# Turning attention outputs by DMA in two f16 halves, and rebuilding 64-bit weights in two VectorE passes

## The chip, the core and the metric

The kernel runs on one NeuronCore of a Trainium2 chip. The core has five engines that run their own instruction streams and meet through semaphores: TensorE (PE in the profile; its weight loads are listed as PEld), VectorE (DVE), ScalarE (ACT), GpSimd (POOL) and SyncE (SP), which here issues all DMAs. Matmul results land in PSUM; GpSimd works on SBUF alone in this kernel. The metric is the device time of one execution in microseconds (us). The kernel before takes 1158.41 us, the median of 3 runs (1158.35 to 1158.62).

## What is computed

Attention with queries pooled in pairs, then a gated feed-forward block that mixes each token with the one before it. B = 8 batches, H = 8 heads, S = 1152 keys, 576 pooled queries, D = 64; the model width is 512 and the inner width 1024.

```
q_pool = q.reshape(B, H, S // 2, 2, D).mean(axis=3)
scores = scale * q_pool @ k^T;  attn = softmax(scores);  x_head = attn @ v
x = concat of heads: (8, 576, 512)
x_prev = x shifted by one token (zero at the start of a batch)
xk = mu_k * x + (1 - mu_k) * x_prev;   xr likewise with mu_r
k = relu(xk @ w_k);  v = k * k @ w_v;  r = sigmoid(xr @ w_r);  out = r * v
```

The weights arrive as 64-bit floats. Every float32 product is made of f16 or bf16 pieces (a high part and a low part), so that a product takes three matmuls.

## The kernel before

**Attention.** There are 64 heads (n = 0 to 63, eight to a batch), each of six blocks of 96 queries. A block (`block`) runs through the engines in turn: 9 score matmuls into one of three PSUM buffers `s` (L479), a maximum on VectorE (L486), a small turn on TensorE (L489), a second maximum (L492), a matmul that spreads it (L494), one row written by ScalarE (L497), 9 more matmuls that add the low parts and the maximum (L503), the exponential on ScalarE (L509) into `pf`, and the low part `pl` by GpSimd (L512). The buffer `s` is free again when the exponential has read it. Five windows to a head (`window`) multiply these by `v` into one PSUM bank `a` (L538, L540, L545); at the last window of a head, bank `a` is divided by the row sums into `xb` (L562 to L569).

**The turn.** The feed-forward needs x with channels on partitions. After every second head, `xb` holds 5 pieces of 128 tokens by 128 channels (two heads). TensorE turns them by a product with the identity in two groups, of 3 and of 2 (L581), back into bank `a`, and ScalarE copies each group into `xt` (L584). `xt` has three buffers, one to a batch in turn; the four pairs of a batch fill its groups g = 0 to 3.

**Feed-forward.** 4608 tokens are worked in 18 tiles of 256 (`ff`). `mix` makes xk and xr from `xt`, one channel group c at a time (ScalarE L653, VectorE L656, ScalarE L662, GpSimd L664); then come the products with w_k, w_r and w_v (all L684), with L711 to L748 behind them. A tile can be worked when all four groups of its tokens stand in `xt`.

**Weights.** In the first stage, beside the attention of batch 0, 20 pieces of 128 by 512 weights are rebuilt from their 64-bit words (`weights`): a DMA of 512 KB into one of two staging buffers `st` (L602), ScalarE's scaled absolute value of the upper words into PSUM bank `f` (L613), three VectorE passes (shift L615, sign L616, low bits L618) that end in `ex`, the f16 high part by ScalarE (L620) and the low part by GpSimd (L621). The first two loads (`iss.nw <= 2`) name `ks1`, `ks2` and `vr` of the first heads as read, so they are issued after those are ready.

**What sets the order.** No instruction is issued as written: `op` records each with its engine, an assumed duration, what it reads and writes and a priority (`key`), and `Issue.run` lists all engines' streams, SP's DMA issues among them, by trying list schedules with these durations. Each engine then works its stream strictly in order. A changed duration or a removed instruction thus moves others anywhere.

Of the kernel before, what the change touches and what calls it, by code (L numbers as in the profile page):

```python
# [34 lines left out]
LO, VLO = 2.0 ** -28, 2.0 ** -12  # L35
# [223 lines left out]
def kernel(  # L259
# [63 lines left out]
    kr, vr = bufs("kr", 2, [P, NC, D], F32), bufs("vr", 2, [P, NC, D], F32)  # L323
# [5 lines left out]
    ks1, ks2 = bufs("ks1_", 2, [P, NC, P], F16), bufs("ks2_", 2, [P, NC, P], F16)  # L329
# [5 lines left out]
    cross = const.tile([P, D + 1], F32, name="cross")  # L335
# [3 lines left out]
    xt = bufs("xt", 3, [P, NG, TQ + 1], F32)  # L339
# [119 lines left out]
    def block(n, j, i, t):  # L459
# [22 lines left out]
        for c0, c1 in BK:  # L482
# [11 lines left out]
        op("PE", 0.05, lambda: nc.tensor.matmul(s[:, 0:QN], mbz[0:QN].broadcast_to([QN, P]),  # L494
                                                 negi[0:QN, 0:QN], start=False, stop=False, skip_group_check=True),
           r=[("mb", z)], w=[("s", z)], key=t + O_MAX)
        op("ACT", 0.133, lambda: nc.scalar.activation(qlo[QN:QN + 1], s[QN:QN + 1, 0:QN], AF.Prelu,  # L497
                                                      scale=1.0 - EPS, alpha=(1.0 + EPS) / (1.0 - EPS)),
           r=[("s", z)] + kl, w=kl, key=t + O_MAX)

# [21 lines left out]
    def window(n, w, t):  # L522
# [32 lines left out]
        if w < NW - 1:  # L555
# [3 lines left out]
        z = n % 2  # L559
        dz, xz = den[z], xb[0]  # L560
        up = slice(HALF, P)
        op("ACT", 0.25, lambda: nc.scalar.activation(cross[up], a_b[0:HALF, 0:VN], AF.Copy, scale=VLO),  # L562
           r=[("a",)], w=[("cross",)], key=t + O_EVAC)
        op("DVE", 0.16, lambda: nc.vector.tensor_tensor(a_b[up, 0:VN], a_b[up, 0:VN], cross[up], op=ALU.add),
           r=[("cross",), ("a",)], w=[("a",)], key=t + O_EVAC)
        op("DVE", 0.075, lambda: nc.vector.tensor_scalar(dz, u[:, :, D], GUARD, None, op0=ALU.add),
           r=[("a",)], w=[("den", z)], key=t + O_EVAC)
# [2 lines left out]
            xz[:, :, hh], u[:, :, 0:D], dz.unsqueeze(2).broadcast_to([P, NW, D]), op=ALU.mult),  # L570
           r=[("den", z), ("a",)], w=[("xb", hh)], key=t + O_EVAC)
        if hh == 0:
            return
        for k0, k1 in TURN:
            q0, qe = spans(k0, k1)
# [10 lines left out]
               r=[("a",)], w=[("xt", b % 3, g, k0)], key=t + O_TURN)  # L586


    def weights(n, w, kc, key, step):
        cols = w.shape[1]  # L590
        wv = w.bitcast(I32).rearrange("(c p) (f t) -> c p f t", p=P, t=2)
        for c in range(kc):
            for f in range(0, cols, 512):
                i = iss.nw = getattr(iss, "nw", 0) + 1
                i %= 2
                s3 = st[i].rearrange("p (f t) -> p f t", t=2)
                wl, wh = s3[:, :, 0], s3[:, :, 1]
# [12 lines left out]
                op("ACT", 0.48, lambda u=u, wh=wh: nc.scalar.activation(u, wh.bitcast(F32), AF.Abs, scale=2.0 ** -111),  # L613
                   r=[ks], w=[kf], key=key)
                v_(0.6, lambda ui=ui: nc.vector.tensor_scalar(ui, ui, 3, None, op0=ALU.logical_shift_left), [kf], [kf])  # L615
# [204 lines left out]
```

## Time and profile before

| | value |
|---|---|
| median of 3 runs | 1158.41 us (1158.35 to 1158.62) |
| the profiled execution itself | 1158.5 us |
| its span, first to last instruction | 1156.7 us (1.8 us lie outside) |
| matmuls | 18928, of which 160 are turns (L581) |
| DMA issued from SP's queue | 123.77 MB, 47.1% of 16 engines' span |
| DMA transposes | 66 of queries, 64 of keys |

The page gives busy time by engine. A matmul's duration in it is longer than the distance to the next one, since matmuls overlap; what one costs in TensorE's stream is read from the starts of neighbours in the timeline. The chain of waits is followed back from the last instruction to what released each step. In rows of groups, `out<-in` gives the tiles, `x` the count, then busy us and mean ns, then the idle time before them and its releasers.

### The profile page before, as it was taken

The numbers are of one execution on the slowest core, as the hardware profiler recorded it, in microseconds if no ns is written. First come the engines' busy times: TensorE is split into PE (matmuls) and PEld (weight loads), VectorE is DVE, ScalarE is ACT, GpSimd is POOL, SyncE is SP. The second block draws the span as 40 slices with busy tenths as digits, with TensorE's granted clock in tenths as the row PEclk, the third lists the DMA queues.
The fourth block names the chain that finished last, engine by engine and source line by source line (L and its number), as shares of the span: only waits on it lengthen the run. The fifth ranks groups of instructions, "written<-read, shape, count | busy, mean of one in ns | idle before, by whom it ended". The sixth has DMA issues, their size and how long they took to land.

```text
span 1156.7 us, 44885 instructions
## 1 busy us (share of the span) xinstructions
PE 1105.0 (96%) x18928; PEld 916.0 (79%) x18928; DVE 859.4 (74%) x1622; ACT 875.9 (76%) x1810; POOL 740.0 (64%) x883
## 2 busy tenths in 40 slices
PE   3878889999999999999999999999999999999998
PEld 3767787988889887978788888879797878887565
DVE  6899987888887777787687878777787778673320
ACT  4778888788778787887878786978887788775643
POOL 3767786766767567666767675857666676654431
PEclk9799999999999999999999999999999999999999
DMA  9687655466354644565444444655544444310000
GB/s 225 183 201 183 172 137 138 99 130 133 99 124 104 126 90 111 124 114 115 93 118 97 116 96 110 119 116 102 114 109 104 111 96 93 73 27 11 19 20 28
DMA packets 222378, 126.64 MB, mean 109 GB/s; under 512 B 157664, under 2 KB 194528, under 8 KB 222176
## 3 DMA queue, kind: packets, MB, share of 16 engines
q1 hardware_dynamic: 222176, 123.77, 47.1%
q8 instruction: 148, 2.42, 0.9%
q14 instruction: 54, 0.44, 0.1%
HBM read 67.11 MB, written 9.44 MB: 66 GB/s over the span
## 4 chain that ended last, share of the span: by engine, by line
PE 85%; DVE 5%; ACT 4%; DMA 3%; issue 2%; SPq 1%; ACTq 0%; DVEq 0%
PE f L684 33%; PE s L479 11%; PE s L503 11%; PE a L538 7%; PE a L540 7%; PE a L545 6%; PE s L684 4%; ACT pf L509 2%; DVE mx L486 2%; PE s L489 2%; PE a L684 2%; PE s L494 1%; PE a L581 1%; DMA ks<-kn 1%; DMA kr<-in_k_dram 1%
## 5 line engine op out<-in xcount | busy, mean ns | idle before, releaser
L486 DVE TENSOR_REDUCE mx<-s 128x96 f16<-128x864 f32 x384 | 401.5, 1054 | 107.2 <-PE s L479 59.8
L512 POOL TENSOR_SCALAR pl<-pf 128x864 f16<-128x864 uint16 (+1 forms) x384 | 337.8, 880 | 186.3 <-ACT pf L509 157.9
L509 ACT ACTIVATE pf<-s 128x864 int32<-128x864 f32 x384 | 337.6, 889 | 84.6 <-PE s L503 50.5
L479 PE MATMUL s<-qT,ks 128*128 128x96 f16 x3456 | 217.8, 208 | 25.6 <-ACT pf L509 12.7
L538 PE MATMUL a<-vt,pf 128*128 128x65 f16 x2880 | 230.2, 194 | 1.5 <-ACT pf L509 0.9
L540 PE MATMUL a<-vt,pf 128*128 128x64 f16 x2880 | 230.4, 194 | 0.0
L479 PEld LDWEIGHTS <-ks 128*128 128x128 f16 x3456 | 185.4, 99 | 51.3 <-issue 18.4
L503 PE MATMUL s<-qT,ks 128*128 128x96 f16 x3456 | 215.0, 208 | 7.5 <-ACT qT L497 6.8
L538 PEld LDWEIGHTS <-pf 128*128 128x128 f16 x2880 | 200.5, 99 | 6.3 <-ACT pf L509 1.2
L503 PEld LDWEIGHTS <-ks 128*128 128x128 f16 x3456 | 181.9, 99 | 28.7 <-issue 9.1
L540 PEld LDWEIGHTS <-pf 128*128 128x128 f16 x2880 | 192.4, 98 | 7.7 <-issue 1.0
L492 DVE TENSOR_REDUCE mb<-s 96x1 f16<-96x128 f32 x384 | 109.3, 285 | 79.9 <-PE s L489 71.8
L497 ACT ACTIVATE qT<-s 1x96 f16<-1x96 f32 x384 | 92.1, 242 | 88.4 <-PE s L494 75.7
L684 PE MATMUL f<-xhk,wk_hi 128*128 128x256 f16 x496 | 135.1, 272 | 0.2
L684 PE MATMUL f<-xlk,wk_hi 128*128 128x256 f16 x496 | 135.1, 272 | 0.0
L684 PE MATMUL f<-xhk,wk_lo 128*128 128x256 f16 x496 | 135.1, 272 | 0.0
L545 PE MATMUL a<-vb,pl 128*128 128x65 f16 x2304 | 124.0, 194 | 0.2 <-POOL pl L512 0.2
L684 PEld LDWEIGHTS <-wk_hi 128*128 128x128 f16 x1152 | 107.0, 98 | 11.0 <-issue 0.4
L435 POOL TENSOR_TENSOR kn<-kr,kn 128x320 f16<-128x320 f32 x126 | 99.6, 802 | 17.5 <-ACT kn L430 13.5
L715 POOL TENSOR_TENSOR gl<-g 128x512 f16<-128x512 f32 x72 | 77.3, 1075 | 46.1 <-ACT g L713 43.8
L545 PEld LDWEIGHTS <-pl 128*128 128x128 f16 x2304 | 99.2, 98 | 5.1 <-POOL pl L512 0.5
L489 PE MATMUL s<-identb,mx 128*96 128x128 f16 x384 | 87.6, 228 | 6.8 <-DVE mx L486 6.7
(96 smaller groups left out, 2089.9 us busy)
## 6 DMA issues: line engine op xcount, KB each, us to landing
kr<-in_k_dram SPq DMA_DIRECT2D x64, 288.0 KB, 3.0
vr<-in_v_dram SPq DMA_DIRECT2D x64, 288.0 KB, 3.2
qr<-in_q_dram SPq DMA_DIRECT2D x32, 320.0 KB, 3.4
ks<-ks SPq DMA_DIRECT2D x64, 144.0 KB, 2.5
out_dram<-em SPq DMA_DIRECT2D x36, 256.0 KB, 2.4
qr<-in_q_dram SPq DMA_DIRECT2D x32, 256.0 KB, 3.3
st<-in_moe_w_k_dram SPq DMA_DIRECT2D x8, 512.0 KB, 4.9
st<-in_moe_w_v_dram SPq DMA_DIRECT2D x8, 512.0 KB, 4.6
```

Source lines behind the costliest of these rows:

```text
L435: lambda cs=cs, en=nc.vector if ve else nc.gpsimd: en.tensor_tensor(kn[i][:, cs, D:P], kr[i][:, cs], kn[i][:, cs, 0:D], op=ALU.subtract),
L479: nc.tensor.matmul(cols(c, c + 1), ks1[hp][:, c, :], qhi, start=(c == c0), stop=False, skip_group_check=True)
L486: op("DVE", 0.967, lambda: nc.vector.tensor_reduce(mxz, grid(0, NC).rearrange("p c q -> p q c"), axis=AX.X, op=ALU.max), r=[("s", z)], w=[ ...
L489: op("PE", 0.054, lambda: nc.tensor.matmul(s[0:QN, 0:P], mxz, identb, start=False, stop=False, skip_group_check=True), r=[("mx", z)], w=[( ...
L492: op("DVE", 0.199, lambda: nc.vector.tensor_reduce(mbz[0:QN], s[0:QN, 0:P], axis=AX.X, op=ALU.max), r=[("s", z)], w=[("mb", z)], key=t + O ...
L503: nc.tensor.matmul(cols(c, c + 1), ks2[hp][:, c, :], qlo, start=False, stop=True, skip_group_check=True)
L509: op("ACT", NC * QN / 1200 + 0.051, lambda: nc.scalar.activation(pf[:, :, HALF + rows.start:HALF + rows.stop], grid(0, NC), AF.Exp, bias=S ...
L512: op("POOL", NC * (r1 - r0) / 1000 + 0.066, lambda: nc.gpsimd.tensor_scalar(to, half(pf, U16, 0)[:, :, HALF + r0:HALF + r1], LO, 1.0, op0= ...
L538: nc.tensor.matmul(a_b[:, a0:a0 + VN], half(pf, F16, 1)[:, c, his], vt[jv][:, c, D:D + VN], start=(w == 0 and c == 0), stop=False, skip_gr ...
L540: nc.tensor.matmul(a_b[:, a0:a0 + D], half(pf, F16, 1)[:, c, his], vt[jv][:, c, 0:D], start=False, stop=(side and c == NC - 1), skip_group ...
L545: nc.tensor.matmul(a_b[:, a0:a0 + VN], pl[:, c, rows], vb[jv][:, c, 0:VN], start=False, stop=(c == NC - 1), skip_group_check=True)
L684: nc.tensor.matmul(ps, terms[i][0], terms[i][1], start=(first and i == 0), stop=(i == last), skip_group_check=True)
```

## The change

Three things are done, and three assumed durations of the planner are set anew (0.133 to 0.36 for L497, 0.25 to 0.34 for L562, 0.16 to 0.36 for L564, and 0.48 to 0.52 for L613).

1. **The turn, from batch 1 on (n >= 8).** ScalarE casts `xb` to an f16 high half, GpSimd makes the f16 rest, two DMA transposes turn the halves, and GpSimd adds them into `xt`. The halves live in the two `st` buffers, which the weights no longer need by then. Batch 0 keeps the turn on TensorE.
2. **The weights.** The shift pass and the pass for the low bits become one; the low bits are taken by ScalarE from the top byte of the lower word. So two VectorE passes and one more ScalarE pass a piece.
3. **Staging.** The weights pass through four buffers, two of them in `xt[2]`, which batch 2 is the first to use; a memset restores its zero column. Pieces 3 and 4 fall into buffers of their own, and their loads have no reads named that hold them back.

```diff
+    xbh, xbl, xth, xtl = (st[i].bitcast(F16)[:, o * NW * P:(o + 1) * NW * P] for i in (0, 1) for o in (0, 1))
...
+        if n >= H:
+            flat = "p k h d -> p (k h d)"
+            op("ACT", 0.63, lambda: nc.scalar.copy(xbh, xz.rearrange(flat)),
+               r=[("xb", 0), ("xb", 1)], w=[("xbh",), *old[0]], key=t + O_TURN)
+            op("POOL", NW * P * 0.0019 + 0.09, lambda: nc.gpsimd.tensor_tensor(xbl, xz.rearrange(flat), xbh, op=ALU.subtract),
+               r=[("xb", 0), ("xb", 1), ("xbh",)], w=[("xbl",), *old[0]], key=t + O_TURN)
+            for kx, x, to in (("xbh", xbh, xth), ("xbl", xbl, xtl)):
+                op("DMA", 0.8, lambda x=x, to=to: nc.sync.dma_start_transpose(to.rearrange("p (k x) -> p k x", k=NW), x),
+                   r=[(kx,)], w=[(kx, "t"), *old[1]], key=t + O_TURN, tail=2.0)
+            op("POOL", TQ * 0.0019 + 0.09, lambda: nc.gpsimd.tensor_tensor(
+                xt[b % 3][:, g, 1:1 + TQ], xth[:, HALF:], xtl[:, HALF:], op=ALU.add),
+               r=[("xbh", "t"), ("xbl", "t")], w=[("xt", b % 3, g, k0) for k0, k1 in TURN], key=t + O_TURN, port=True)
+            return
...
+    far = xt[2].rearrange("p c t -> p (c t)").bitcast(I32)
+    stage = [*st, *(far[:, i * 1024:(i + 1) * 1024] for i in range(2))]
...
-                i %= 2
-                s3 = st[i].rearrange("p (f t) -> p f t", t=2)
+                i, j = i % 2, i % len(stage)
+                s3 = stage[j].rearrange("p (f t) -> p f t", t=2)
+                tops = stage[j].bitcast(U8).rearrange("p (f b) -> p f b", b=8)[:, :, 3]
...
-                   r=[("ks1", 1, 0), ("ks2", 0), ("vr", 1)] if iss.nw <= 2 else [], w=[ks], key=key, tail=4.5)
+                   r=[("ks1", 1, 0), ("ks2", 0), ("vr", 1)] if iss.nw <= 2 else [], w=[ks, kl], key=key, tail=4.5)
...
-                v_(0.6, lambda ui=ui: nc.vector.tensor_scalar(ui, ui, 3, None, op0=ALU.logical_shift_left), [kf], [kf])
-                v_(0.6, lambda ui=ui, wh=wh: nc.vector.scalar_tensor_tensor(
-                    ui, wh, -0x80000000, ui, op0=ALU.bitwise_and, op1=ALU.bitwise_or), [ks, kf], [kf])
-                v_(0.6, lambda ei=ei, ui=ui, wl=wl: nc.vector.scalar_tensor_tensor(
-                    ei, wl, 29, ui, op0=ALU.logical_shift_right, op1=ALU.bitwise_or), [ks, kf], [ke])
+                    op("ACT", 0.57, lambda wl=wl, tops=tops: nc.scalar.activation(wl, tops, AF.Copy, bias=-0.49, scale=2.0 ** -5),
+                       r=[ks, kl], w=[kl], key=key)
+                    v_(0.6, lambda ui=ui, wl=wl: nc.vector.scalar_tensor_tensor(
+                        ui, ui, 3, wl, op0=ALU.logical_shift_left, op1=ALU.bitwise_or), [kl, kf], [kf])
+                    v_(0.6, lambda ei=ei, ui=ui, wh=wh: nc.vector.scalar_tensor_tensor(
+                        ei, wh, -0x80000000, ui, op0=ALU.bitwise_and, op1=ALU.bitwise_or), [ks, kf], [ke])
...
+    op("POOL", 0.2, lambda: nc.gpsimd.memset(xt[2][:, :, 0:1], 0.0), w=[(m, j) for m in ("st", "sl") for j in (2, 3)] +
+       [("xt", 2, g, k0) for g in range(NG) for k0, k1 in TURN], key=W_REST * PER + 14 * W_REST_STEP * PER)
```

With these lines in place the line numbers of the changed kernel run ahead by 3 at the attention (L486 becomes L489) and by 25 at the feed-forward (L684 becomes L709).

Three places show how instructions move. The first is SP's stream at the program's start, before:

```order
L392 DMA qr_74<-in_q_dram 128x5x128
L423 DMA kr_70<-in_k_dram 128x576
L423 DMA kr_71<-in_k_dram 128x576
L392 DMA qr_74<-in_q_dram 128x4x128
L423 DMA vr_72<-in_v_dram 128x576
L423 DMA vr_73<-in_v_dram 128x576
L364 DMA mu_k<-in_moe_mu_k_dram 128x4x1
L364 DMA mu_r<-in_moe_mu_r_dram 128x4x1
```

and of the change, at the same place:

```order
L395 DMA qr_74<-in_q_dram 128x4x128
L426 DMA vr_72<-in_v_dram 128x576
L426 DMA vr_73<-in_v_dram 128x576
L622 DMA xt_105<-in_moe_w_k_dram 128x1024
L622 DMA st_121<-in_moe_w_k_dram 128x1024
L367 DMA mu_k<-in_moe_mu_k_dram 128x4x1
L367 DMA mu_r<-in_moe_mu_r_dram 128x4x1
L395 DMA qr_74<-in_q_dram 128x5x128
L416 DMA_TRANSPOSE qT_83<-qn_78 128x5x128
```

Two weight loads of 512 KB (into the spare `xt` and a staging buffer) now stand between the first heads' loads and `mu_k`, ahead of every transpose; before, the first weight load stood behind the first six transposes.

The second place is TensorE's stream behind the last head, where the last pair is turned while the feed-forward goes on; before:

```order
L684 LDWEIGHTS xlr
L684 MATMUL f<-wr_hi,xlr 128x512
L581 MATMUL a<-ident,xb_102 128x128 x3
L684 LDWEIGHTS xr
L684 MATMUL f<-wr_hi,xr 128x512
```

and of the change:

```order
L709 LDWEIGHTS xlr
L709 MATMUL f<-wr_hi,xlr 128x512
L709 LDWEIGHTS xr
L709 MATMUL f<-wr_hi,xr 128x512
L709 LDWEIGHTS xr
L709 MATMUL f<-wr_lo,xr 128x512
```

The turns are gone from between the feed-forward's matmuls, and with them the writes into bank `a`.

The third place is GpSimd's stream at the end of batch 2, where the fourth pair of heads is turned. Only the change has rows for the turn here: the rest `xbl` (written to `st`) and the sum into `xt`.

```order
L455 TENSOR_SCALAR vb_90<-vr_72 128x9x64
L515 TENSOR_SCALAR pl<-pf 128x9x96
L581 TENSOR_TENSOR st_121<-xb_102,st_121 128x640
L515 TENSOR_SCALAR pl<-pf 128x9x96 x3
L586 TENSOR_TENSOR xt_105<-st_122 128x576
L515 TENSOR_SCALAR pl<-pf 128x9x96
L515 TENSOR_SCALAR pf<-pf 128x9x64
```

Between the two new instructions, while the transposes are under way, GpSimd has three blocks' low parts to make; the sum stands ahead of the next ones.

More of the change, by code (lines that the diff above doesn't have):

```diff
@@ L16 @@
 U16 = mybir.dt.uint16
+U8 = mybir.dt.uint8
 AF = mybir.ActivationFunctionType
@@ L347 @@
     st = bufs("st", 2, [P, 1024], I32)
+    xbh, xbl, xth, xtl = (st[i].bitcast(F16)[:, o * NW * P:(o + 1) * NW * P] for i in (0, 1) for o in (0, 1))
+    old = [[(m, i) for m in ("st", "sl")] for i in (0, 1)]
     whi, wlo = {}, {}
@@ L496, in block @@
            r=[("mb", z)], w=[("s", z)], key=t + O_MAX)
-        op("ACT", 0.133, lambda: nc.scalar.activation(qlo[QN:QN + 1], s[QN:QN + 1, 0:QN], AF.Prelu,
+        op("ACT", 0.36, lambda: nc.scalar.activation(qlo[QN:QN + 1], s[QN:QN + 1, 0:QN], AF.Prelu,
                                                       scale=1.0 - EPS, alpha=(1.0 + EPS) / (1.0 - EPS)),
@@ L561, in window @@
         up = slice(HALF, P)
-        op("ACT", 0.25, lambda: nc.scalar.activation(cross[up], a_b[0:HALF, 0:VN], AF.Copy, scale=VLO),
+        op("ACT", 0.34, lambda: nc.scalar.activation(cross[up], a_b[0:HALF, 0:VN], AF.Copy, scale=VLO),
            r=[("a",)], w=[("cross",)], key=t + O_EVAC)
-        op("DVE", 0.16, lambda: nc.vector.tensor_tensor(a_b[up, 0:VN], a_b[up, 0:VN], cross[up], op=ALU.add),
+        op("DVE", 0.36, lambda: nc.vector.tensor_tensor(a_b[up, 0:VN], a_b[up, 0:VN], cross[up], op=ALU.add),
            r=[("cross",), ("a",)], w=[("a",)], key=t + O_EVAC)
@@ L600, in weights @@
                 hi, lo = whi[n][:, c, f:f + 512], wlo[n][:, c, f:f + 512]
-                ke, ks = ("ex", i), ("st", i)
+                ke, ks, kl = ("ex", i), ("st", j), ("sl", j)
                 op("DMA", 0.36, lambda s3=s3, src=wv[c, :, f:f + 512]: nc.sync.dma_start(s3, src),
-                   r=[("ks1", 1, 0), ("ks2", 0), ("vr", 1)] if iss.nw <= 2 else [], w=[ks], key=key, tail=4.5)
+                   r=[("ks1", 1, 0), ("ks2", 0), ("vr", 1)] if iss.nw <= 2 else [], w=[ks, kl], key=key, tail=4.5)
                 def v_(dur, fn, r, w):
@@ L612, in weights @@
                 ui = u.bitcast(I32)
-                op("ACT", 0.48, lambda u=u, wh=wh: nc.scalar.activation(u, wh.bitcast(F32), AF.Abs, scale=2.0 ** -111),
+                op("ACT", 0.52, lambda u=u, wh=wh: nc.scalar.activation(u, wh.bitcast(F32), AF.Abs, scale=2.0 ** -111),
                    r=[ks], w=[kf], key=key)
-                v_(0.6, lambda ui=ui: nc.vector.tensor_scalar(ui, ui, 3, None, op0=ALU.logical_shift_left), [kf], [kf])
-                v_(0.6, lambda ui=ui, wh=wh: nc.vector.scalar_tensor_tensor(
-                    ui, wh, -0x80000000, ui, op0=ALU.bitwise_and, op1=ALU.bitwise_or), [ks, kf], [kf])
-                v_(0.6, lambda ei=ei, ui=ui, wl=wl: nc.vector.scalar_tensor_tensor(
-                    ei, wl, 29, ui, op0=ALU.logical_shift_right, op1=ALU.bitwise_or), [ks, kf], [ke])
+                if True:
+                    op("ACT", 0.57, lambda wl=wl, tops=tops: nc.scalar.activation(wl, tops, AF.Copy, bias=-0.49, scale=2.0 ** -5),
[4 more added lines that the diff above has]
+                        ei, wh, -0x80000000, ui, op0=ALU.bitwise_and, op1=ALU.bitwise_or), [ks, kf], [ke])
+                else:
+                    v_(0.6, lambda ui=ui: nc.vector.tensor_scalar(ui, ui, 3, None, op0=ALU.logical_shift_left), [kf], [kf])
+                    v_(0.6, lambda ui=ui, wh=wh: nc.vector.scalar_tensor_tensor(
+                        ui, wh, -0x80000000, ui, op0=ALU.bitwise_and, op1=ALU.bitwise_or), [ks, kf], [kf])
+                    v_(0.6, lambda ei=ei, ui=ui, wl=wl: nc.vector.scalar_tensor_tensor(
+                        ei, wl, 29, ui, op0=ALU.logical_shift_right, op1=ALU.bitwise_or), [ks, kl, kf], [ke])
                 op("ACT", 0.52, lambda hi=hi, e=e: nc.scalar.copy(hi, e), r=[ke], w=[("w", n, c, f)], key=key)
```

## The prediction

> **What bounds the kernel now.** First the page's busy times, then the same engines by stage (columns: window, length, busy us and instructions of PE, PEld, DVE, ACT, POOL, then granted clock, DMA share, GB/s), then the chain of waits of the long middle stage by line.
>
> ```profile
> PE 1105.0 (96%) x18928; PEld 916.0 (79%) x18928; DVE 859.4 (74%) x1622; ACT 875.9 (76%) x1810; POOL 740.0 (64%) x883
> ...
> 0.00:14.00 14.00, 2.34 (x27) 2.13 (x27) 9.74 (x28) 6.35 (x13) 4.94 (x13) 1.00 0.85 211
> 14.00:160.00 146.00, 114.72 (x2242) 102.74 (x2243) 127.78 (x240) 110.17 (x223) 101.17 (x117) 0.91 0.74 182
> 160.00:1060.00 900.00, 895.14 (x16059) 754.35 (x16057) 699.05 (x1311) 716.00 (x1485) 606.98 (x721) 1.00 0.48 105
> 1060.00:1156.70 96.70, 92.81 (x610) 56.80 (x606) 22.84 (x45) 43.39 (x90) 26.95 (x33) 1.00 0.06 23
> ...
> by line: PE f L684 39.5%; PE s L503 13.2%; PE s L479 13.2%; PE a L538 8.2%; PE a L540 8.1%; PE a L545 6.8%; PE s L489 2.1%; PE s L494 1.7%; PE a L581 1.5%; issue 0.9%; DVE mx L486 0.8%; ACT pf L509 0.8%; DMA ks<-kn 0.6%; DVE mb L492 0.3%; A
> ```
>
> From 160 us on the kernel is TensorE's: 895 of 900 us busy, and the shares of PE on the chain add up to 94.3%; waits are at most 5.7%, 51 us. VectorE (78%), ScalarE (80%) and GpSimd (67%) have room. From 14 to 160 us, where batch 0 has no feed-forward beside it, VectorE is the busiest, 127.8 of 146 us (88%), and TensorE has gaps. So a matmul removed behind 160 us is worth its distance to the next one; before that VectorE and ScalarE set the pace; in the first 14 us, arrivals.
>
> **A. The turns go (28 pairs, 140 matmuls, all behind 160 us).** The timeline of TensorE around one pair shows what they cost (start, duration):
>
> ```profile
> 407.11 0.49 PE L581 MATMUL a<-ident,xb 128*128 128x128 f32 x3
> 407.44 0.38 PE L684 MATMUL f<-wv_lo,g 128*128 128x512 f16 x1
> ...
> 408.69 0.40 PE L581 MATMUL a<-ident,xb 128*128 128x128 f32 x2
> 408.93 0.27 PE L684 MATMUL f<-xhk,wk_hi 128*128 128x256 f16 x1
> ...
> L581 PE MATMUL a<-ident,xb 128*128 128x128 f32 x135 | 24.3, 278 | 0.1
> ```
>
> Starts are 0.33 us apart for three and 0.24 for two: 0.57 us a pair, 28 x 0.57 = 16.0 us. The chain says less: 1.5% of 900 us is 13.5 us for the 135 turns of that stage, or 14.0 for 140. I take 15, with 14 and 16 as ends. It is nearly sure, as the next busiest engine there has 20% free.
>
> What takes their place, by the nearest rows:
>
> ```profile
> L715 POOL TENSOR_TENSOR gl<-g 128x512 f16<-128x512 f32 x72 | 77.3, 1075 | 46.1 <-ACT g L713 43.8
> L397 ACT ACTIVATE qn<-qs 128x640 f16<-128x640 f32 x32 | 23.4, 732 | 1.7 <-DVE qs L394 1.4
> L584 ACT COPY xt<-a 128x320 f32<-128x320 f32 x32 | 13.7, 427 | 5.5 <-PE a L581 5.1
> L584 ACT COPY xt<-a 128x256 f32<-128x256 f32 x32 | 11.9, 372 | 0.8 <-PE a L581 0.5
> ...
> 10.37 1.20 SPq L413 DMA_TRANSPOSE qT<-qn  x1
> ...
> qT<-qn SPq DMA_TRANSPOSE x66, 3.4
> ```
>
> ScalarE loses two copies (0.80 us a pair) and gains one cast (0.73): nothing. GpSimd gains a difference of 640 and a sum of 576 elements, by L715's 1.075 us for 512 some 1.34 + 1.21 = 2.55 us a pair, 71 us in all; its 607 us of the middle stage become 678 of about 885 (77%). SP issues two transposes of 1.2 us a pair, and they land 3.4 us after issue. The DMA share of 0.48 would be 0.60 at most if all of it were transposes (280 pieces of 128 on 1152). All this lies beside TensorE; the turn takes longer, but nothing needs it at once.
>
> [...]
>
> [...]
>
> ```profile
> 1064.90 0.45 PE L545 MATMUL a<-vb,pl 128*128 128x65 f16 x9
> ...
> 1067.29 0.49 DVE L569 TENSOR_TENSOR xb<-a,den 128x320 f32<-128x320 f32 x1
> ...
> L653 ACT ACTIVATE tmp<-xt,omu_k 128x256 f32<-128x256 f32 x48 | 23.7, 506 | 3.6 <-DVE xk L656 1.6 <-DVE xr L656 1.6
> L656 DVE SCALAR_TENSOR_TENSOR xk<-xt,mu_k,tmp 128x256 f32<-128x256 f32 x48 | 29.6, 627 | 2.1 <-ACT tmp L653 1.8
> L662 ACT CAST xhk<-xk 128x256 f16<-128x256 f32 x72 | 27.2, 402 | 1.6 <-PE f L684 0.8 <-PE s L684 0.4
> L664 POOL TENSOR_TENSOR xlk<-xk,xhk 128x256 f16<-128x256 f32 x72 | 48.8, 687 | 19.7 <-ACT xhk L662 16.5 <-DVE mx L486 0.4
> ...
> 1137.27 10.36 PE s L684 x48
> ...
> 551.61 2.40 PE f L684 x22
> ```
>
> In the new order 55 matmuls of 512 columns and 32 of 256 stand between the last window and the first one that needs channel group 3: at 10.36/48 = 0.216 and 2.40/22 = 0.109 us that is 15.4 us of cover. The path is 2.6 (from the window's end at 1065.2 to `xb` at 1067.8) + 0.73 + 1.34 + 3.4 + 1.21 + 2.2 for mixing (the four rows above: 0.51 + 0.63 + 0.40 + 0.69) = 11.5 us, which leaves 3.9 us for eight handovers. It fits: no cost.
>
> **B. The first 14 us.** The order lets two weight loads of 512 KB in ahead of `mu_k`. VectorE works in order, and there it waits for `mu_k`; the maximum of the first block comes behind.
>
> ```profile
> 2.76 0.98 SPq L423 DMA_DIRECT2D vr<-in_v_dram  x2
> ...
> 3.78 4.99 DMA mu_k<-in_moe_mu_k_dram
> ...
> 8.80 0.24 DVE L366 TENSOR_SCALAR omu_k<-mu_k 128x4 f32<-128x4 f32 x1 [2.66 <-DMA mu_k<-in_moe_mu_k_dram]
> ...
> 13.72 2.01 DVE L486 TENSOR_REDUCE mx<-s 128x96 f16<-128x864 f32 x2
> ...
> GB/s 0 14 225 381 327 326 378 210 277 176 244 92 93 213 199 217 207 112 90 246 197 378 389 292 228 297 327 278 90 171 337 285 267 105 278 391 294 166 44 43
> ```
>
> The chain ran through this wait, and VectorE has no idle time from 8.80 to the first maximum. 1.05 MB more in the same queue takes 3.2 us at the 327 GB/s of 2 to 7 us (1 us a slice), 5.0 at the mean of 211 in the first 14. The least is 1.0 us for the two issues (L423's two took 0.98). I take +3; nothing later gives it back, since the stage behind it is full.
>
> **C. 14 to 160 us.** 20 pieces lose one VectorE pass each and ScalarE gains one.
>
> ```profile
> L615 DVE TENSOR_SCALAR f<-f 128x512 int32<-128x512 int32 x20 | 13.8, 692 | 0.9 <-ACT f L613 0.7
> L613 ACT ACTIVATE f<-st 128x512 f32<-128x512 f32 x20 | 12.8, 641 | 1.1 <-DMA st<-in_moe_w_v_dram 0.8
> ...
> 157.08 0.27 PE L684 MATMUL f<-xhk,wk_hi 128*128 128x256 f16 x1
> ```
>
> VectorE: 127.8 - 13.8 = 114.0 us. ScalarE, priced by its other pass over the same words: 110.2 + 12.8 = 123.0. The busiest engine falls from 127.8 to 123.0; if the stage keeps its density, 146 x 123.0/127.8 = 140.5, a gain of 5.5 us. The ends: all 13.8 if VectorE alone set the pace, 0 if ScalarE, which now has three passes a piece between the blocks' exponentials, holds what VectorE gives. I take 5.5. The first feed-forward matmul starts at 157.08; in the new order it stands behind 52 blocks' first scores instead of 56, which fits.
>
> **D. Crowding behind 160 us.** GpSimd's 71 us are 12% more of its work; 12% of the 51 us of waits would be 6. Below nothing: bank `a` is free sooner, and the windows' first matmuls (L538) waited 0.4 us for the copies out of it. VectorE's mixing, all shapes of the middle stage, has a wide spread (ns least/median/most):
>
> ```profile
> L538 PE MATMUL a<-vt,pf 128*128 128x65 f16 x2880 | 230.2, 194 | 1.5 <-ACT pf L509 0.9 <-ACT xt L584 0.4
> ...
> L656 DVE SCALAR_TENSOR_TENSOR xk<-xt,mu_k,tmp x83: 270/473/1310, 180.2 to 1042.3; 128x256 f32<-128x256 f32 x36, 128x192 f32<-128x192 f32 x16, 128x128 f32<-128x128 f32 x16, 128x64 f32<-128x64 f32 x15
> ```
>
> The longest takes 1.31 us where 256 columns take 0.63 on average, so something holds it up at times; more GpSimd work may make that more. I take +1.5, since both engines have over 20% free. [...]
>
> **Sum.** 1158.5 (the profiled execution: 1156.7 span + 1.8 around it, 0.1 over the median of the runs) - 15 + 3 - 5.5 + 1.5 = 1142.5 us.
>
> **The rivals.**
>
> *Slower: GpSimd waits for the transposes.* GpSimd works in order, and the sum into `xt` stands ahead of later blocks' low parts; while it waits, these wait, and TensorE's windows behind them. At the end of batch 2 only three blocks' low parts are between.
>
> ```profile
> 11.56 2.34 PE L479 MATMUL s<-qT,ks 128*128 128x96 f16 x27 [11.56 <-DMA ks<-kn]
> ...
> L512 POOL TENSOR_SCALAR pl<-pf 128x864 f16<-128x864 uint16 (+1 forms) x384 | 337.8, 880 | 186.3 <-ACT pf L509 157.9
> ```
>
> For it: three low parts are only 2.6 us of work, and a landing takes 3.4 and a second issue 1.2. Against it: GpSimd already idles 157.9 us for exponentials, so low parts come at the pace of blocks, from the first scores at 11.56 to the last window at 1065, 1053/384 = 2.7 us each, and three of them cover 8 us; most pairs have five or more instructions between. It decides from 16/28 = 0.57 us lost a pair; at 1.5 us a pair the time is 1142.5 + 42 = 1184, at 1 us 1170.5. 8%.
>
> *ScalarE takes VectorE's place.* C is 0: 1158.5 - 15 + 3 + 1.5 = 1148, and with the worse ends of A, B and D (-14, +5, +6) 1155.5. For it: 123 against 127.8 us is a small step, and ScalarE's work sits on every block's path. 20%.
>
> *VectorE alone was the brake.* C is the whole 13.8: 1134, with the other ends (-16, +1, 0) 1129.7. 8%.
>
> *The turns were free.* If they only filled waits, A is 0: 1157.5. Against it: 94.3% of the chain on PE. 4%.
>
> **How the numbers follow.** The forecast, 1142.5, has 60% (C between 3 and 10, about 1136 to 1149). The range reaches over the second and third rivals: 1130 to 1156, which leaves out the first and fourth and a little of the rest. A measurement of this kernel can tell 0.2% (2.3 us) from no change. Faster by more: the forecast, the second and third rivals, 88%. Slower by more: the first, 8%. The same: the fourth, 4%.
>
> **What would show it.** A: 18788 matmuls, no gap where the turns were, PE still at 99% of the middle stage; wrong if waits of GpSimd on transposes or of PE on `pl` appear. B: `mu_k` lands at about 12 us and the first maximum starts near 16.7; wrong if it starts at 14. C: the first feed-forward matmul, 157.1 now, near 150 with B in it; wrong if ScalarE's busy share nears 95% and it comes at 158 or later. D: the chain's share of waits behind 160 us stays under 7%.

## The result and the profile after

The changed kernel takes 1131.52 us, the median of 4 runs (1130.22 to 1134.1), beside 1158.51 us for the kernel before in the same series. The ratio is 0.9765, with a 95% interval of 0.9742 to 0.9787: by the ratio 27.2 us less, where 16 were forecast. The direction held and the range (1130 to 1156) held at its edge; the size was too small.

The page's head and first queue after (busy us, share of the span, instructions; for the queue: packets, MB, share of 16 engines):

```profile
span 1129.7 us, 44739 instructions
...
PE 1082.7 (96%) x18788; PEld 896.3 (79%) x18788; DVE 867.5 (77%) x1602; ACT 887.4 (79%) x1802; POOL 818.7 (72%) x940
...
q1 hardware_dynamic: 259808, 132.96, 56.2%
```

The 140 turns are gone from TensorE. GpSimd is busy 79 us longer and is still the least busy engine; the queue moves 9 MB more. By stage, in the columns used before:

```profile
0.00:14.00 14.00, 0.00 (x0) 0.00 (x0) 6.82 (x25) 6.90 (x14) 4.58 (x13) 1.00 0.93 264
14.00:160.00 146.00, 121.39 (x2437) 109.64 (x2437) 130.24 (x240) 129.78 (x259) 108.60 (x126) 0.94 0.83 188
160.00:1060.00 900.00, 895.49 (x15956) 747.75 (x15953) 716.22 (x1316) 721.39 (x1474) 686.06 (x779) 1.00 0.56 115
1060.00:1129.70 69.70, 65.86 (x401) 38.94 (x398) 14.22 (x24) 29.28 (x57) 19.43 (x24) 1.00 0.06 23
```

The middle stage looks as it did: TensorE 99.5% busy. The first stage holds more work of every engine than before, ScalarE 129.8 us instead of 110.2, and TensorE's granted clock is 0.94 instead of 0.91.

**Where the time went.** To split the gain I set each matmul down with the distance between starts that its kind has when it runs back to back (for the main kinds 0.0425 us for 96 columns, 0.030 for a window's, 0.109 for 256, 0.216 for 512, 0.112 for one turn of 128), and call **lost** whatever a matmul's start lies behind the sum of those ahead of it. A matmul that runs at a lower clock thus counts as partly lost, too. This is worked out from all matmul starts of the trace, up to the last one; it is no view of the profile. In us:

| | work of all matmuls | lost by 40 | lost by 160 | lost by 200 | lost after 200 |
|---|---|---|---|---|---|
| before | 1056.7 | 28.4 | 74.8 | 75.7 | 20.2 |
| after | 1041.0 | 28.4 | 65.0 | 66.2 | 18.4 |
| difference | -15.7 | 0.0 | -9.8 | -9.5 | -1.8 |

So 15.7 of the 27.0 us between the two profiles are the turns, 9.5 come from the first stage, all of it between 40 and 160 us, and 1.8 from the rest.

### The profile page after: what moved, and what is told of

It is laid out like the page before. It is cut to its first block, busy times and chain, and to the rows that moved or that the text cites. A ratio compares the mean times of both kernels' runs of the same rounds, so it can differ in the third digit from the quotient of the medians.

```text
span 1129.7 us, 44739 instructions
## 1 busy us (share of the span) xinstructions
PE 1082.7 (96%) x18788; PEld 896.3 (79%) x18788; DVE 867.5 (77%) x1602; ACT 887.4 (79%) x1802; POOL 818.7 (72%) x940
## 4 chain that ended last, share of the span: by engine, by line
PE 88%; DVE 4%; ACT 3%; issue 2%; DMA 1%; POOL 1%; SPq 0%; ACTq 0%; DVEq 0%; POOLq 0%
PE f L709 35%; PE s L482 12%; PE s L506 11%; PE a L541 7%; PE a L543 7%; PE a L548 6%; PE s L709 4%; PE s L492 2%; DVE mx L489 2%; PE a L709 2%; PE s L497 1%; ACT pf L512 1%; DMA mu_k<-in_moe_mu_k_dram 0%; DVE vt L452 0%; DVE mb L495 0%
## 5 line engine op out<-in xcount | busy, mean ns | idle before, releaser
L489 DVE TENSOR_REDUCE mx<-s 128x96 f16<-128x864 f32 x384 | 400.7, 1053 | 98.1 <-PE s L482 46.9
L482 PEld LDWEIGHTS <-ks 128*128 128x128 f16 x3456 | 183.6, 99 | 48.7 <-DMA ks<-kn 14.4
L506 PEld LDWEIGHTS <-ks 128*128 128x128 f16 x3456 | 179.2, 99 | 21.6 <-issue 3.1
L709 PE MATMUL f<-xhk,wk_hi 128*128 128x256 f16 x496 | 135.1, 272 | 0.3 <-ACT r L736 0.3
L709 PE MATMUL f<-xlk,wk_hi 128*128 128x256 f16 x496 | 135.1, 272 | 0.0
L709 PE MATMUL f<-xhk,wk_lo 128*128 128x256 f16 x496 | 135.1, 272 | 0.0
L709 PEld LDWEIGHTS <-wk_hi 128*128 128x128 f16 x1152 | 105.9, 98 | 10.4 <-issue 0.4
L438 POOL TENSOR_TENSOR kn<-kr,kn 128x320 f16<-128x320 f32 x126 | 96.4, 776 | 8.9 <-ACT kn L433 3.4
```

The costliest lines, as they stand in the source:

```text
L438: lambda cs=cs, en=nc.vector if ve else nc.gpsimd: en.tensor_tensor(kn[i][:, cs, D:P], kr[i][:, cs], kn[i][:, cs, 0:D], op=ALU.subtract),
L482: nc.tensor.matmul(cols(c, c + 1), ks1[hp][:, c, :], qhi, start=(c == c0), stop=False, skip_group_check=True)
L489: op("DVE", 0.967, lambda: nc.vector.tensor_reduce(mxz, grid(0, NC).rearrange("p c q -> p q c"), axis=AX.X, op=ALU.max), r=[("s", z)], w=[ ...
L506: nc.tensor.matmul(cols(c, c + 1), ks2[hp][:, c, :], qlo, start=False, stop=True, skip_group_check=True)
L709: nc.tensor.matmul(ps, terms[i][0], terms[i][1], start=(first and i == 0), stop=(i == last), skip_group_check=True)
```

## The experiments

Two readings stood against each other. One: each part has its own price (turns -15.7, passes about -9, staging and durations about nothing), and the parts add up. The other: the first stage's gain belongs to the new order of all instructions as much as to any one part, since each edit makes the planner list the whole program anew. In the table, and in the text below, a gain in us is the ratio's distance from 1 times 1158.5; b_ is the kernel before with one part alone, a_ the change with one part undone; the granted clock is the window's 14 to 160 us, and lost times are worked out as above.

| kernel | passes | ratio to before in its series (95%) | lost by 200 | lost after 200 | clock |
|---|---|---|---|---|---|
| before | 3 | 1 | 75.7 | 20.2 | 0.91 |
| b_turn | 3 | 0.9916 (0.9896 to 0.9936) | 81.2 | 21.7 | 0.89 |
| b_stage | 3 | 1.0069 (1.0042 to 1.0096) | 81.2 | 21.5 | 0.92 |
| b_dur | 3 | 0.9990 (0.998 to 1.000) | 74.3 | 22.2 | 0.93 |
| b_plan | 3 | 1.0038 (1.0021 to 1.0055) | 78.8 | 22.4 | 0.92 |
| a_3pass | 3 | 0.9848 (0.9830 to 0.9867) | 77.4 | 19.6 | 0.89 |
| b_pass | 2 | 0.9950 (0.9934 to 0.9966) | 70.9 | 20.7 | 0.92 |
| a_2stage | 2 | 0.9881 (0.9861 to 0.9901) | 75.6 | 23.8 | 0.84 |
| a_olddur | 2 | 0.9823 (0.980 to 0.9847) | 74.4 | 18.5 | 0.91 |
| a_gate4 | 2 | 0.9808 (0.9782 to 0.9834) | 68.8 | 22.0 | 0.92 |
| a_plan | 2 | 0.9759 (0.9737 to 0.9781) | 64.5 | 20.0 | 0.95 |
| after | 2 | 0.9765 (0.9742 to 0.9787) | 66.2 | 18.4 | 0.94 |

### One part alone

**b_turn: the turn by DMA alone** (three passes, two staging buffers and the old durations kept).

```diff
+        if n >= H:
+            op("ACT", 0.63, lambda: nc.scalar.copy(xbh, xz.rearrange(flat)),
...
```

> The kernel before with the turn by DMA alone (three passes, two staging buffers, the old durations). Theory 'parts add up': 140 matmuls of 0.11 us go, 15.7 us less work on TensorE, and its lost time (the time its stream is not at work, 95.9 us before and 84.6 in the change) stays near 96: 1143 us. Rival 'bank a': the turn also frees the bank sooner and saves waits, and the lost time behind 160 us falls by the change's 1.5 us or more: 1141 or less. Rival 'plan': the gain rests on the new durations, and without them waits on the transposes eat a part: 1147 or more.

It gained 0.84%, 9.7 us. Matmul work fell by the whole 15.7 us, but 5.5 more were lost by 200 us and 1.5 after. The edit touches nothing in the first 160 us except the order, and by 160 us no more was lost than before (74.7 for 74.8). The loss comes behind that: the first feed-forward matmul starts at 166.6 instead of 157.1, with 60 blocks' first scores ahead of it instead of 56. The time is that of the rival 'plan', but not by its reason: GpSimd waited for transposes three times, 4.8 us in all, and TensorE never for a low part. So the turn is worth what it takes out of TensorE's stream, and the new order gave some 6 us of that back.

**b_pass: the two passes alone.**

```diff
-                v_(0.6, lambda ui=ui: nc.vector.tensor_scalar(ui, ui, 3, None, op0=ALU.logical_shift_left), [kf], [kf])
+                    op("ACT", 0.57, lambda wl=wl, tops=tops: nc.scalar.activation(wl, tops, AF.Copy, bias=-0.49, scale=2.0 ** -5),
+                       r=[ks, kl], w=[kl], key=key)
...
```

> The kernel before with two VectorE passes and one more ScalarE pass a piece, nothing else. Theory 'parts add up': the lost time up to 160 us falls by about 7 of the change's 9.8 us: 1151 us. Rival 'staging': without spare buffers the loads wait for the passes as before, and ScalarE is only fuller: 1157 to 1160. Rival 'plan': the new durations made the first stage's gain: no change, 1158.

It gained 0.50%, 5.8 us, of which 4.8 were won by 200 us. The first stage of this kernel, first to 160 us and then to the exponential of its 54th block, at 153.0 us (156.3 before):

```profile
14.00:160.00 146.00, 117.18 (x2328) 106.39 (x2326) 123.61 (x232) 126.55 (x255) 106.82 (x123) 0.92 0.80 192
```

```profile
14.00:153.00 139.00, 110.18 (x2193) 99.72 (x2191) 117.52 (x220) 121.44 (x245) 100.53 (x115) 0.91 0.81 194
```

ScalarE is now the busiest engine. To 160 us it has almost the 127.8 us that VectorE had before, but by then this kernel has done more of the work. To the same point of the program ScalarE has 121.4 us, where VectorE had 124.9 of 142.3: if the busiest engine sets the length at the old density, 142.3 x 121.4/124.9 = 138.3 us. It took 139.0. With the passes alone, the prediction's rule comes out.

**b_stage: the four staging buffers alone.**

```diff
-                i %= 2
+                i, j = i % 2, i % len(stage)
+                s3 = stage[j].rearrange("p (f t) -> p f t", t=2)
...
```

> The kernel before with four staging buffers and the two ungated early loads, nothing else. Theory 'parts add up': loads were not what the passes waited for (1.1 us of idle time before ScalarE's first pass), so no gain, and the early loads cost 1.6 us at the first maximum that is made good by the fourth block: 1158 to 1160. Rival 'staging': the spare buffers take the loads out of the way of the keys' and queries' transposes: 1153 or less.

It is slower, by 0.69% or 8.0 us, which neither reading expected; 5.5 are lost by 200 us. Its first exponential starts at 21.6 us instead of 17.8, but by the fourth block it is ahead (29.5, 29.8). The loss comes later in the stage, and what makes it was not found.

**b_dur: the new durations alone.**

```diff
-        op("ACT", 0.133, lambda: nc.scalar.activation(qlo[QN:QN + 1], s[QN:QN + 1, 0:QN], AF.Prelu,
+        op("ACT", 0.36, lambda: nc.scalar.activation(qlo[QN:QN + 1], s[QN:QN + 1, 0:QN], AF.Prelu,
...
```

> The kernel before with the four new durations in the planner alone; the work is the same. Theory 'parts add up': within the spread of plans, 1155 to 1162. Rival 'plan': the truer load of ScalarE lets the planner order the first stage better: the lost time up to 160 us falls by 5 us or more, 1153 or less.

No change that can be told. Added up, the four parts alone give -9.7 - 5.8 + 8.0 - 1.2 = -8.7 us. The whole gives -27.2: **the parts do not add.**

### One part undone

**a_3pass: the change with three passes.**

```diff
-                if True:
+                if False:
```

> The change with the old three VectorE passes a piece (turn by DMA, four buffers and new durations kept). Theory 'passes': the lost time up to 200 us belongs with those of three passes so far (74.3 to 81.2) and not with those of two (66.2 to 74.4): about 76, 1141 us. Rival 'durations or staging': it stays near 66 to 69, and the passes bring nothing: 1131 to 1135.

9.6 us of the 27.2 go (ratio 0.9848 for 0.9765), and lost by 200 us is 77.4 again, 11.2 more than in the change. That is what the theory 'passes' expected. Without the second edit nothing of the first stage's gain is left.

**a_2stage: the change with two staging buffers.**

```diff
-    stage = [*st, *(far[:, i * 1024:(i + 1) * 1024] for i in range(2))]
+    stage = [*st]
```

> The change with two staging buffers as before (turn by DMA, two passes and new durations kept). Theory 'passes': the lost time up to 200 us belongs with those of two passes, 66 to 74, whatever the buffers: 1128 to 1139 us. Rival 'staging': two passes need the spare buffers, and it goes to 75 or more: 1140 or more.

Here 13.4 us go, the most of any part that was undone, though the same buffers cost 8.0 alone; in its trace 9.4 are lost by 200 us and 5.4 behind it. The first stages of the two kernels with a part undone, a_3pass first:

```profile
14.00:160.00 146.00, 115.64 (x2228) 103.72 (x2229) 128.74 (x242) 108.83 (x219) 99.64 (x116) 0.89 0.74 181
```

```profile
14.00:160.00 146.00, 120.19 (x2273) 110.21 (x2274) 119.65 (x220) 122.00 (x242) 100.44 (x115) 0.84 0.74 184
```

With three passes VectorE is full and ScalarE has room, as before. With two buffers neither is full (82% and 84%), but the granted clock is the lowest of all, 0.84. The section on the hardware comes back to it.

**a_olddur: the change with the old durations.**

```diff
-        op("ACT", 0.36, lambda: nc.scalar.activation(qlo[QN:QN + 1], s[QN:QN + 1, 0:QN], AF.Prelu,
+        op("ACT", 0.133, lambda: nc.scalar.activation(qlo[QN:QN + 1], s[QN:QN + 1, 0:QN], AF.Prelu,
...
```

> The change with the four old durations in the planner. Theory 'parts add up': within the spread of plans, 1129 to 1136. Rival 'plan': without the truer ScalarE durations the lost time up to 160 us rises by 5 us or more: 1137 or more.

6.7 us go, all in the first stage, as the rival 'plan' had it, although no engine executes anything else than in the change. **Order alone is worth this much.**

**a_gate4: the first four weight loads held back** until the first heads are ready, so that `mu_k` does not stand behind two of them.

```diff
-                   r=[("ks1", 1, 0), ("ks2", 0), ("vr", 1)] if iss.nw <= 2 else [], w=[ks, kl], key=key, tail=4.5)
+                   r=[("ks1", 1, 0), ("ks2", 0), ("vr", 1)] if iss.nw <= 4 else [], w=[ks, kl], key=key, tail=4.5)
```

> The change with the first four weight loads, not two, held back until the first heads' keys and values are ready. Theory: mu_k lands about 2.7 us sooner (near 8.8), and the first maximum starts near 13.7 instead of 15.3, but the blocks behind are bound by VectorE and ScalarE and by what they wait for from DMA, so by the fourth block nothing of it is left: 1130 to 1133. Rival (the prediction's step): what the start loses stays lost: 1128 to 1129.5.

The start was sooner (first exponential at 18.1 us, not 19.7; 27.5 us lost by 40, not 28.4), and the time 5.0 us longer, which neither reading expected. What the start saved was not kept; but this kernel has another order throughout, so the run doesn't show why.

### The same work in another order

**a_plan and b_plan: the change and the kernel before with other numbers of the planner.**

```diff
-PLANS = ((0.08, 0.1), (0.12, 0.15))
+PLANS = ((0.07, 0.09), (0.11, 0.14))
```

> The change with the planner's two margins for lateness a hundredth lower, which gives other orders for the same work. The seeds of the run before last had given the very same order, so they told nothing of plans. Theory 'plans scatter': the lost time up to 200 us, 66.2 in the change, moves by 2 to 6 us either way, and the whole by as much: 1128 to 1140. Rival 'the edits set it': it stays within 1.5 us of 66.2, and the time within 3 us of 1131.5.

> The kernel before with the same two margins a hundredth lower. Theory 'plans scatter': the lost time up to 200 us (75.7 before; 81.2 with the turn alone, which does not touch the first stage's work) comes out between 72 and 82; the time between 1155 and 1167. Rival 'the edits set it': within 1.5 us of 75.7.

The change stays where it was, and the kernel before becomes 4.4 us slower. So the gain is there in a second pair of orders, too: in these it is 32 us.

**a_seed and b_seed: another start of the planner's trials.**

```diff
-        trials = [times(LATE, SLACK, 1 + i) for i in range(3)]
+        trials = [times(LATE, SLACK, 11 + i) for i in range(3)]
```

> The change with other random draws in the planner's trials: the same work in another of the orders that it tries. It measures how far the time moves by the choice of a plan alone: if by 3 us or more, differences of a few us between the other runs say nothing of the edits.

> The kernel before with other random draws in the planner's trials, as in the run on the change: the spread by the choice of a plan alone; 1155 to 1162 is expected, and the lost time up to 160 us between 72 and 78 us.

Both trials ended in the very order that the kernels had, so these runs say nothing of other orders. They repeat the two kernels: ratios 0.9764 and 0.9993, and 68.0 and 74.6 us lost by 200 where the first profiles had 66.2 and 75.7. So a lost time is good to about 2 us.

### What follows from all of them

Lost by 200 us averages 78.1 us in the six kernels with three passes (74.3 to 81.2) and 70.1 in the six with two (64.5 to 75.6). The difference, 8.0 us, is the best figure here for what two passes are worth in the first stage; the groups overlap, and the two pairs that differ in the passes alone give 4.8 us (before and b_pass) and 11.2 us (a_3pass and after). The same work of this stage in other orders spreads over 7 us (before, b_turn, b_dur and b_plan: 74.3 to 81.2) and 10 us (after, a_plan and a_olddur: 64.5 to 74.4). The change stands at the good end of its group, the kernel before on the good side of its own. Staging changes its sign with what stands beside it, and the durations their size (1.2 us alone, 6.7 in the change). No run undoes the turn alone. Whether four buffers help because VectorE then needs the weights sooner, or because this order happens to suit them, is not settled: there is one order for each combination.

## Why the prediction was right in sign and short in size

**A, the turns: right.** 15 was forecast (14 to 16). By the distances above 140 turns are 15.7 us of work. That is a price and no measurement, but the kernel got it whole: behind 200 us, where nearly all of them had stood, no more was lost than with the old turn (18.4 for 20.2; D below). What took the turns' place, in three views: the middle stage by groups (count, busy us, mean ns, idle before and its releaser), the waits of GpSimd in the whole run (us, times, longest), and the transposes' landing (median us):

```profile
L548 PE MATMUL a<-vb,pl 128*128 128x65 f16 x1980 | 106.9, 193 | 0.0
...
L581 POOL TENSOR_TENSOR st<-xb,st 128x640 f16<-128x640 f32 x28 | 41.5, 1483 | 12.1 <-ACT st L579 11.0
L586 POOL TENSOR_TENSOR xt<-st 128x576 f32<-128x576 f16 x28 | 36.6, 1307 | 7.7 <-DMA st<-st 6.0
L579 ACT CAST st<-xb 128x640 f16<-128x640 f32 x28 | 20.2, 722 | 1.7 <-DVE xb L572 1.3
```

```profile
POOL pl L515 <- ACT pf L512: 86.0, 110, 2.8
...
POOL st L581 <- ACT st L579: 11.0, 9, 5.1
...
POOL xt L586 <- DMA st<-st: 6.0, 2, 4.3
```

```profile
st<-st SPq DMA_TRANSPOSE x56, 3.4
```

The sizes were close: 1.48 + 1.31 us of GpSimd a pair for 1.34 + 1.21, 0.72 for 0.73 on ScalarE, 3.4 for 3.4 to land. GpSimd's waits for exponentials fell from 157.9 to 86.0 us: the new work went into them. **The slower rival fell.** The waits that it named did appear: of 28 sums two waited for a transpose, 6.0 us together, and nine of the subtractions for their cast, 11.0 us. But they stayed GpSimd's own: where 0.57 us a pair lost to TensorE would have decided, its windows never waited for a low part in the middle stage (0.0). The DMA's transpose is the slower of the two (3.4 us to land, 0.49 for three turns before), but its 3.4 us lie beside a TensorE that had no time to spare.

The program's end also fitted, where three tiles wait for the last pair's group. GpSimd there (start, duration, idle before it):

```profile
1038.25 1.40 POOL L581 TENSOR_TENSOR st<-xb,st 128x640 f16<-128x640 f32 x1 [5.11 <-ACT st L579]
1043.97 1.48 POOL L586 TENSOR_TENSOR xt<-st 128x576 f32<-128x576 f16 x1 [4.33 <-DMA st<-st]
```

The longer of the two waits for a transpose, 4.33 us, and the longest for a cast, 5.11 us, are the last pair's, with no block left to work on; TensorE's feed-forward matmuls start without a gap (0.11 or 0.22 us apart) from 1039.7 to 1050 beside it.

**B, the first 14 us: the delay was there, but it did not stay.** VectorE's start:

```profile
11.43 0.17 DVE L369 TENSOR_SCALAR omu_k<-mu_k 128x4 f32<-128x4 f32 x1 [5.27 <-DMA mu_k<-in_moe_mu_k_dram]
...
15.31 2.02 DVE L489 TENSOR_REDUCE mx<-s 128x96 f16<-128x864 f32 x2
```

and the load that it waited for, its issue and then its size and its time from issue to landing:

```profile
5.75 0.43 SPq L367 DMA_DIRECT2D mu_k<-in_moe_mu_k_dram  x1
...
mu_k<-in_moe_mu_k_dram SPq DMA_DIRECT2D x1, 2.0 KB, 5.7
```

The wait for `mu_k` is 5.27 us where it was 2.66, and it ends 2.6 us later. Of these, 2.0 are the later issue (5.75 for 3.78); the landing took only 0.7 longer (5.7 for 5.0; over all kernels 5.7 to 6.6 with the loads ahead and 5.0 to 5.6 without), so the 1.05 MB ahead of it in the queue did not hold it for the 3.2 to 5.0 us of the prediction. With 1.0 us less of VectorE's work between, the first maximum starts 1.6 us later, not 3 (the forecast was 16.7). Then the fourth block's exponential starts at 28.8 us, 1.0 sooner than before, and by 40 us nothing is lost. The step that failed is "nothing later gives it back". That it came back because the loads ahead of `mu_k` were of weights that the stage needed anyway is a guess; a_gate4, which saved the start, ended slower, in another order.

**C, 14 to 160 us: the direction was right, the size was not.** -5.5 was forecast and with B's +3 came to -2.5; lost time fell by 9.5 to 9.8. So 3 us of the difference are B's, which did not last, and some 4 are C's. To the same point of the program, the exponential of the 54th block (156.3 us before, 147.5 after), before first:

```profile
14.00:156.30 142.30, 111.03 (x2168) 99.19 (x2169) 124.89 (x235) 106.92 (x218) 97.72 (x114) 0.90 0.75 186
```

```profile
14.00:147.50 133.50, 108.89 (x2211) 97.84 (x2212) 119.49 (x222) 117.80 (x233) 97.52 (x113) 0.94 0.85 195
```

ScalarE's new pass costs nearly what its neighbour does (0.68 us for L630's 0.64), and VectorE's two cost what they did (0.69 and 0.68 for 0.68 to 0.69; stage 14 to 160 us; one row of two, for the pieces in `xt[2]`):

```profile
L635 DVE SCALAR_TENSOR_TENSOR f<-f,xt 128x512 int32<-128x512 int32 x10 | 6.9, 693 | 0.5 <-ACT f L630 0.4
...
L637 DVE SCALAR_TENSOR_TENSOR ex<-xt,f 128x512 int32<-128x512 int32 x10 | 6.8, 676 | 0.0
...
L633 ACT ACTIVATE xt<-xt 128x512 int32<-128x512 uint8 x9 | 6.1, 681 | 0.1
```

So the prices were right. The loads came out otherwise in part. ScalarE has 117.8 us to this point, about what the new passes add up to; but VectorE, which was to fall behind it, is still the busiest. It lost 13.8 us of passes and took on 8.4 of other work in this stretch (3.8 more for `vt`, of which 17 pieces fall into it for 14, and 2.1 and 2.0 for `xk` and `qs`).

The failed step is **"if the stage keeps its density"**. VectorE has 119.5 us for 124.9: at the old density that is 142.3 x 119.5/124.9 = 136.1 us, 6.2 less, close to the 5.5. The other 2.6 us are density: VectorE is busy 89.5% of the stretch for 87.8%, with ScalarE at 88% beside it for 75%. And density is nothing that a stage keeps. To the 54th block, the busiest engine has 87.3 to 91.3% in the six kernels with three passes and 83.4 to 89.5% in the six with two; each per cent is some 1.5 us. The highest is that of b_dur, where only the order differs from the kernel before:

```profile
14.00:154.10 140.10, 110.88 (x2207) 97.74 (x2205) 127.86 (x236) 108.13 (x219) 97.77 (x114) 0.93 0.78 190
```

So the load alone gives 4.0 us in b_pass and 6.2 here, near the forecast; how densely an order packs the stage can be worth as much. Before, the chain of waits of this stage ran through 19.6 us of three landings (start, duration),

```profile
19.64 8.33 DMA kr<-in_k_dram
...
78.07 5.66 DMA qT<-qn
...
105.14 5.62 DMA ks<-kn
```

which belong to loads and not to the passes; afterwards only 3.4 us of landings are on it, but 19 us of "issue" (time for which the profile shows no wait) for 14. It is tempting to take the closed gaps for the gain, but landings do not tell good orders from bad ones. b_turn, with three passes, has a single long one on its chain and lost as much by 160 us; the kernel before in its other profile (b_seed) has 22.0 us of others. b_turn first:

```profile
20.43 8.15 DMA kr<-in_k_dram
```

```profile
17.65 6.84 DMA vr<-in_v_dram
103.31 5.50 DMA ks<-kn
129.18 5.13 DMA vr<-in_v_dram
135.73 4.57 DMA qT<-qn
```

What makes one order denser than another, and whether two passes leave the order more room, no run shows. The first feed-forward matmul came at

```profile
137.30 0.27 PE L709 MATMUL f<-xhk,wk_hi 128*128 128x256 f16 x1
```

where the forecast had near 150. Of these 20 us, the four blocks fewer that it stands behind are 10, at 2.5 us a block before ((156.3 - 141.2)/6, from the 48th to the 54th). The second rival (ScalarE takes VectorE's place, C = 0) fell with b_pass (4.8 us) and a_3pass (11.2). The third (all 13.8) is nearer in its total, 1134, than the forecast, but it needs a ScalarE with room to spare, and at 88% beside VectorE's 89.5% that is not what the stage shows.

**D, crowding behind 160 us: not there.** +1.5 was forecast. Eight traces with the DMA turn lost 18.4 to 23.8 us after 200 (mean 20.3), six with TensorE's turn 20.2 to 22.4 (mean 21.4). GpSimd's extra 79 us took nothing from the end that can be measured. The chain from 160 to 1030 us:

```profile
by line: PE f L709 41.7%; PE s L482 13.8%; PE s L506 13.5%; PE a L541 8.2%; PE a L543 8.1%; PE a L548 6.8%; PE s L492 2.2%; PE s L497 1.8%; issue 0.8%; DVE mx L489 0.6%; ACT pf L512 0.5%; DVE vt L452 0.2%; ACT tmp L678 0.2%; DVE qs L397 0.2
```

PE's shares add up to 96.1%, 94.3% before, so waits are under 4%. The longest mixing of `xk` on VectorE is 1.57 us for 1.31, that of `xr` 1.17 for 1.29, and both medians are the same 0.47. That GpSimd's work is what holds a mixing up was a guess, and no run shows it.

In sum: -15.7 for -15, -9.5 for -2.5, -1.8 for +1.5. B, C and D all erred to the same side. The time lies outside the 1136 to 1149 that had 60%, and 1.5 us inside the range, which reached so far down for the third rival, whose mechanism is not what was found: that it held is partly luck. Passes alone account for 5 to 11 of the 9.5, 8 on average; which part of the rest is staging, durations or a good order stays open.

## What to carry to other kernels

Where one engine is busy 99% of a long stage, price an operation by what it takes out of that engine's stream, and let the replacement be several times longer, provided that something stands between its issue and its use: here 0.57 us of TensorE a pair were exchanged for some 8 us of cast, subtraction, second issue, landing and sum, and TensorE waited for none of it. Where two engines share a stage, compare stretches that end at the same point of the program and not at the same time, and don't take the density for fixed: scaling by the busiest engine gave 138.3 us for b_pass's 139.0, but 136.1 for the change's 133.5. And where a planner lists everything anew, test a part in several orders before pricing it: the same work spread over 7 to 10 us here, as much as most parts are worth.

## What the runs showed of the hardware

**TensorE's granted clock falls to half at times in the first stage.** TensorE in the kernel before, around 50 us (start, duration), and by two windows (length, busy us and counts as above, then the granted clock):

```profile
48.83 0.24 PE L538 MATMUL a<-vt,pf 128*128 128x65 f16 x1
48.88 0.24 PE L540 MATMUL a<-vt,pf 128*128 128x64 f16 x1
48.94 0.25 PE L538 MATMUL a<-vt,pf 128*128 128x65 f16 x1
...
49.16 0.91 PE L503 MATMUL s<-qT,ks 128*128 128x96 f16 x9
...
50.18 0.19 PE L540 MATMUL a<-vt,pf 128*128 128x64 f16 x1
50.20 0.19 PE L538 MATMUL a<-vt,pf 128*128 128x65 f16 x1
50.23 0.19 PE L540 MATMUL a<-vt,pf 128*128 128x64 f16 x1
...
53.06 0.54 PE L503 MATMUL s<-qT,ks 128*128 128x96 f16 x9
```

```profile
44.00:49.00 5.00, 4.09 (x54) 3.62 (x52) 4.99 (x10) 2.97 (x7) 3.75 (x5) 0.50 0.72 156
50.00:54.00 4.00, 4.00 (x123) 4.00 (x121) 2.67 (x4) 3.19 (x7) 3.11 (x4) 1.00 0.39 82
```

The same matmuls start 0.055 us apart and then 0.025 to 0.03, nine score matmuls take 0.91 us and then 0.54, and the granted clock is 0.50 and then 1.00. By longer windows, before and after:

```profile
40.00:60.00 20.00, 15.88 (x288) 14.03 (x287) 17.74 (x34) 15.47 (x33) 15.56 (x20) 0.83 0.56 155
```

```profile
40.00:60.00 20.00, 15.56 (x318) 13.27 (x319) 19.01 (x37) 19.13 (x38) 16.47 (x19) 1.00 1.03 236
```

TensorE is as busy as before in those 20 us (15.6 us for 15.9) and gets 10% more matmuls done, at a full clock. How busy it was before a fall can be counted, as the traces' record of the clock goes in pieces of 3.41 us (or several of them), each at 1.00 or at 0.50 in the kernels before and after. Two pieces at full clock in the kernel before, of which the first was followed by half clock and the second was not:

```profile
39.69:43.10 3.41, 1.43 (x21) 1.03 (x20) 3.23 (x6) 3.31 (x9) 3.08 (x4) 1.00 0.79 243
70.41:73.82 3.41, 2.10 (x54) 1.97 (x54) 2.81 (x6) 3.08 (x5) 3.17 (x5) 1.00 0.92 216
```

TensorE was busy 42% of the first and 62% of the second. In all 14 traces, from the first fall to 160 us, 49 pieces at full clock were followed by half clock, with TensorE busy 33 to 68% of them, and 371 were not, busy 49% or more: above 68% none lost it. At half clock 40 pieces, busy 30 to 87%, were followed by half clock again, and 62, busy 78 to 100%, by full. So TensorE need not stand still to lose the clock; what makes it fall, no run shows. This is counted from all clock records and matmuls of the traces, with the profile's busy time; it is no view.

Among the two-pass kernels lost time follows the clock without an exception (0.95: 64.5; 0.94: 66.2; 0.92: 68.8 and 70.9; 0.91: 74.4; 0.84: 75.6), among the three-pass ones it does not. At clocks of 0.91 and 0.92 the two groups have 71.4 and 78.6 us on average, still 7.2 apart with three kernels each, so the groups' difference is not the clock's alone. An estimate of what the clock itself takes: if it is either half or full, as in those records, 0.91 and 0.94 on average over 146 us are some 26 and 18 us at half, and a TensorE at work in all of that would lose 13 and 9 us of it, so by this estimate some 4 of the 9.5 us would be directly the clock's. Whether a low clock costs time there or only shows a stage with gaps was not tried: no run sets the clock.

**The first weights landed later with four buffers.** DMA issues of the changed kernel (count, size, median us from issue to landing):

```profile
xt<-in_moe_w_k_dram SPq DMA_DIRECT2D x4, 512.0 KB, 6.4
st<-in_moe_w_k_dram SPq DMA_DIRECT2D x4, 512.0 KB, 5.6
...
qT<-qn SPq DMA_TRANSPOSE x66, 3.9
```

The eight loads of `w_k` took 4.9 us before, and 4.3 (b_turn) to 5.1 (b_pass) in the kernels with two buffers; in those with four, the two halves took 4.9 to 6.4. Whether that is because more of them are under way beside the first heads' loads was not tried. The queries' transposes, 3.9 us here, took 3.4 before and, with four buffers as well, 3.4 in b_stage. The last weights show no such difference (3.9 to 4.7 us for `w_v`, 4.6 before).
